# Handing a PSUM bank from one row tile to the other: GpSimd's empty instruction in place of SyncE's, and no weight split queued in the last six steps before it

## The chip, the cores and the metric

The kernel runs on one core of one Trainium2 chip. The metric is device time in microseconds (us); before the change it is 1293.22 us, the median of 3 runs (1291.1 to 1293.64). Five engines matter here: PE (TensorE, matmuls), DVE (VectorE), ACT (ScalarE), POOL (GpSimd) and SP (SyncE, which issues DMAs). Each takes its instructions in order; they wait for each other by semaphores.

## The reference

x is 2048 x 512; there are 32 heads of 16 with one shared key and value head, and a feed-forward net of width 1376. A gate mixes the two.

```python
g = _sigmoid((x * gate_w).sum(-1, keepdims=True))
q = (x @ wq) in 32 heads of 16;  k = x @ wk;  v = x @ wv     # one k and v for all heads
a = softmax(q k^T / 4) v, heads side by side, @ wo
b = (_gelu(x @ w_gate) * (x @ w_up)) @ w_down
return g * a + (1 - g) * b
```

## The kernel before

**Two streams of work on PE.** After a prologue (some 80 us: queries, keys, values), PE's order is written out by hand in `PLAN` (L45 to L108), one line for each job of the feed-forward net (`f`) or of the output projection (`w`). The letters interleave a job with attention. `S` and `Z` are scores: `scores` (L730) issues two matmuls into a pair of PSUM banks (L744), and ACT makes the exponential of the pair (L747). `Z` uses the third pair, which is also the bank of a job's first product `z`. `V` is the product of one step's probabilities with the values (`pv`, L809, matmuls in L815). `H` begins a job, `F` is one step of it, `R` ends it, `T` sends tanh to ACT.

**A job.** It makes two products at once, `z` and `y` (gate and up for a chunk of 128 of the 1376 columns, or two row blocks of the down or output projection). Every operand stands as a high and a low half, so a product has three terms for each piece of the contraction: a gate job has 12 terms, a down job 15 or 18, a `w` job 12. `pair_mm` (L509) walks through the terms twice: in the first half `z` takes rows 0 to 63 of each term and `y` rows 64 to 127, in the second half the other way round. So one step is two matmuls on the two row tiles of the array, side by side. There are 61 jobs: 39 gate jobs, 16 down jobs and 6 `w` jobs.

**The handover.** Between the halves each bank passes from one row tile to the other. PE must not begin the second half on a bank before the first half's matmuls have written it, so L522 to L526 put an empty instruction, the relay, on another engine: it waits (`after`, L506) for the last two matmuls of the first half, and the first two matmuls of the second half wait for it (L517, L518). It stands on SP. Whatever SP has been given earlier comes first in SP's queue.

**What SP issues in these stretches:** the weight loads of `fetch` (L345, `nc.sync.dma_start` in L349, 256 KB each into one of `STAGE` = 4 stage buffers `st`), the next query tile (`load_q`, L375: four DMAs in L367 and L368 and two in L373, called in L739 at the third key step of a unit), the reloads in L572 and the output (L628).

**Splits.** A weight part that has landed in `st` is split into halves by `split_part` (L352, L186, L187): VectorE casts the high half (`gh`, `dh`, `xh`), GpSimd subtracts it from the part (`gl`, `dl`, `xl`), and `fetch` then orders the next load, which needs a stage buffer that an earlier subtraction has freed. A gate job queues its parts in `todo` (`begin`, L578): two of the gate and up weights for a later job and one or two of the down weights, in the first jobs one of `wo` as well. The end of the last gate job of a row group queues four parts of x.

**Slots.** After every third step (`EVERY` = 3) `slot` (L490) takes one piece of waiting work into the instruction streams: with its argument true, the first of `todo`, or else the first of `bg`; with false, of `bg` alone. `bg` holds VectorE's work on finished attention units (`norm`, L750). In the first half all slots may take a split; in the second half there are slots up to four steps before its end.

Of the kernel before, what the change touches and what calls it, by code (L numbers as in the profile page):

```python
# [111 lines left out]
def mix_kernel(ctx, tc, xT, wq, wo, wf, out):  # L112
    nc = tc.nc
# [376 lines left out]
    def slot(split_too):  # L490
        for q in (todo, bg) if split_too else (bg,):
            if q:
                return q.pop(0)()
# [12 lines left out]
    def after(ins, name):  # L506
        tc.add_manual_dep(ins, name, SYNC, reason="a bank passes from one row tile to the other")

    def pair_mm(z, y, X, Y):  # L509
        for half in range(2):  # L510
            for q in range(len(X)):
                for j, (ps, (a, b)) in enumerate(((z, X[q]), (y, Y[q]))):
                    lower = (j + half) % 2
                    rs = slice(64 * lower, 64 * lower + 64)
                    mm = nc.tensor.matmul(ps, a[rs], b[rs], start=(half == 0 and q == 0),  # L515
                                          stop=(half == 1 and q == len(X) - 1), skip_group_check=True)
                    if half == 1 and q == 0:  # L517
                        after(mm.ins, relay[0])  # L518
                    if half == 0 and q == 0 and j == 0:
                        behind = [None, None]  # L520
                    behind[j] = mm.ins.name
                if half == 0 and q == len(X) - 1:  # L522
                    relay = nc.sync.nop(nofuse=True).ins  # L523
                    for name in behind:
                        after(relay, name)
                    relay = [relay.name]  # L526
                if q % EVERY == EVERY - 1 and (half == 0 or q + 4 <= len(X)):
                    slot(True)
                yield

    def weights_terms(n, t):
# [302 lines left out]
    def play(word, job):  # L834
        if job:
            X, Y = job[0]()
        for t in word.split():
            k = int(t[1:] or 1)
            if t[0] in "SZ":
                for _ in range(k):  # L840
                    score(t[0] == "Z")
            elif t[0] == "V":
                visit(k)
            elif t[0] == "T":
                advance(2)()
                for k, m in ((2, 1), (3, 0)):
                    defer(k, advance(m))
            elif t[0] == "H":
                advance(1)()
                z = two_banks("z", 2)[:, 0:TG]  # L850
                y = ps_f.tile([P, TG], F32, tag="pf", name="y")
                pairs = pair_mm(z, y, X, Y)
            elif t[0] == "F":
                for _ in range(k):
                    next(pairs)
            else:
                assert next(pairs, None) is None
                job[1](z, y)
# [72 lines left out]
```

## Time and profile before

| | before |
|---|---|
| time, median of 3 runs | 1293.22 us |
| the profiled execution | 1292.77 us |
| its span, first to last instruction | 1291.0 us |
| PE matmul busy | 1243.3 us |
| ACT busy | 1029.8 us |
| DVE busy | 571.1 us |
| POOL busy | 220.3 us |
| mean granted TensorE clock | 0.984 |

A row of a group of instructions gives line, engine, operation, output<-inputs and count, then busy time and the mean of one in ns, then the idle time of the engine ahead of them and what ended it. A row of the time line gives start and duration in us, and the idle time before it in brackets. SPq and POOLq are the sequencers of SP and GpSimd, which wait and issue. An empty instruction appears as EVENT_SEMAPHORE in its line, L523. A row of a view by stretches of time gives the stretch, its length, the busy time and count of each engine (PE, weight loads PEld, then DVE, ACT, POOL where they are not left out), the mean granted clock, and two numbers on the DMAs. The end of a matmul is modelled: a next one starts before the shown end of the one ahead.

### The profile page before, as it was taken

The page shows a single profiled execution, that of the slowest core. Times are in us where ns is not written, and L with a number is a line of the kernel's source. Part 1 is how long each engine was busy: PE and PEld are TensorE (multiplying, and loading weights), DVE is VectorE, ACT ScalarE, POOL GpSimd, SP SyncE. Part 2 cuts the span into 40 slices and gives each one's busy share as a digit, 9 for nine tenths or more (in the row PEclk, how much of TensorE's full clock was granted, in tenths as well). Part 3 has the DMA queues.
Part 4 walks back from the last instruction along what each step waited for, and adds up shares of the span by engine and source line. Part 5 has one row for each costly group of instructions (what it writes and reads, how often), then busy time and mean ns, then how long its engine had stood idle before and what let it go on. Part 6 is the DMA issues. An engine that isn't in the chain of part 4 may idle for free.

```text
span 1291.0 us, 23739 instructions
## 1 busy us (share of the span) xinstructions
PE 1243.3 (96%) x9742; PEld 683.6 (53%) x9742; DVE 571.1 (44%) x812; ACT 1029.8 (80%) x1127; POOL 220.3 (17%) x188
## 2 busy tenths in 40 slices
PE   9999999998999999999998999998999999999998
PEld 7864455545545545445554555455455544555555
DVE  7764423554246241264526234064635336053623
ACT  5448888777888878898787888887788888887883
POOL 5423101212022010121212011022202021012100
PEclk9999999989999999999999999999999999999999
DMA  8532101212021010111211121012212021012000
GB/s 317 204 125 66 52 7 50 62 39 79 9 77 49 30 55 22 38 46 42 79 55 46 39 63 31 22 50 63 63 39 63 30 71 47 1 47 60 17 1 33
DMA packets 39839, 73.91 MB, mean 57 GB/s; under 512 B 5488, under 2 KB 5744, under 8 KB 39728
## 3 DMA queue, kind: packets, MB, share of 16 engines
q1 hardware_dynamic: 39184, 71.32, 18.1%
q8 instruction: 77, 1.26, 0.4%
q0 software_dynamic: 256, 0.79, 0.2%
q14 instruction: 34, 0.28, 0.1%
q10 hardware_dynamic: 288, 0.26, 0.1%
HBM read 57.41 MB, written 14.94 MB: 56 GB/s over the span
## 4 chain that ended last, share of the span: by engine, by line
PE 69%; issue 16%; SPq 3%; POOL 1%; DVE 1%; POOLq 0%
PE acc L815 29%; PE s L744 17%; PE z L515 16%; PE y L515 7%; SPq L373 1%; POOL gl L187 1%; SPq L367 1%; SPq L368 1%; SPq L349 1%; PE wos L501 1%; DVE dh L186 0%; DVE acc L627 0%; POOL dl L187 0%; PE wof L501 0%; DVE gh L186 0%
## 5 line engine op out<-in xcount | busy, mean ns | idle before, releaser
L747 ACT ACTIVATE p<-s 128x1024 f32<-128x1024 f32 x1024 | 976.7, 1026 | 201.8 <-PE s L744 189.8
L815 PE MATMUL acc<-p,v 128*32 128x512 f32 x4096 | 484.8, 597 | 0.0
L744 PE MATMUL s<-Q,kp 51*128 51x512 f32 x2048 | 390.4, 421 | 1.5 <-DMA Q<-scr 1.4
L744 PEld LDWEIGHTS s<-Q,kp 51*128 51x128 f32 x2048 | 187.4, 187 | 218.7 <-ACT p L747 124.0
L187 POOL TENSOR_TENSOR gl<-st,gh 128x512 fp32r<-128x512 f32 x80 | 112.3, 1423 | 919.7 <-PE s L744 708.8
L815 PEld LDWEIGHTS acc<-p,v 128*32 128x32 f32 x4096 | 114.0, 109 | 250.2 <-issue 240.6
L515 PE MATMUL z<-xh,gh 64*128 64x512 f32 x312 | 131.4, 421 | 37.3 <-SPq L523 37.3
L515 PE MATMUL y<-xh,gh 64*128 64x512 f32 x312 | 131.3, 421 | 0.0
L515 PE MATMUL y<-xl,gh 64*128 64x512 f32 x312 | 127.5, 409 | 0.0
L515 PE MATMUL z<-xl,gh 64*128 64x512 f32 x312 | 127.4, 408 | 0.0
L515 PE MATMUL z<-xh,gl 64*128 64x512 f32 x312 | 126.8, 406 | 0.0
L515 PE MATMUL y<-xh,gl 64*128 64x512 f32 x312 | 126.8, 406 | 0.0
L541 DVE COPY gs<-z 128x512 f32<-128x512 f32 x39 | 27.0, 692 | 225.2 <-PE y L515 128.6
L515 PEld LDWEIGHTS z<-xh,gh 64*128 64x128 f32 x312 | 61.1, 196 | 56.6 <-SPq L523 47.8
L515 PE MATMUL z<-dh,hh 64*128 64x512 f32 x176 | 70.2, 399 | 3.7 <-SPq L523 3.7
L515 PE MATMUL y<-dh,hh 64*128 64x512 f32 x176 | 70.1, 398 | 0.0
L515 PE MATMUL y<-dl,hh 64*128 64x512 f32 x176 | 69.4, 394 | 0.0
L515 PE MATMUL z<-dl,hh 64*128 64x512 f32 x176 | 69.4, 394 | 0.0
L515 PE MATMUL z<-dh,hl 64*128 64x512 f32 x176 | 69.2, 393 | 0.0
L515 PE MATMUL y<-dh,hl 64*128 64x512 f32 x176 | 69.2, 393 | 0.0
L515 PEld LDWEIGHTS z<-xh,gl 64*128 64x128 f32 x312 | 60.8, 195 | 11.2
L515 PEld LDWEIGHTS z<-xl,gh 64*128 64x128 f32 x312 | 61.4, 197 | 9.8
(173 smaller groups left out, 1498.2 us busy)
## 6 DMA issues: line engine op xcount, KB each, us to landing
st<-wf SPq DMA_DIRECT2D x125, 256.0 KB
scr<-q SPq DMA_DIRECT2D x16, 512.0 KB
Q<-scr SPq DMA_DIRECT2D x64, 128.0 KB
Q<-scr SPq DMA_DIRECT2D x64, 64.0 KB
out<-acc SPq DMA_DIRECT2D x16, 256.0 KB
xr<-xT SPq DMA_DIRECT2D x6, 512.0 KB
st<-xT SPq DMA_DIRECT2D x12, 256.0 KB
xr<-xT SPq DMA_DIRECT2D x4, 256.0 KB
```

What stands on the lines that cost most here:

```text
L187: eng_l.tensor_sub(lo, src, hi)
L349: nc.sync.dma_start(t, source(*p))
L367: nc.sync.dma_start(t[64 * j : 64 * j + 32].bitcast(F32), rows[0:32, hs])
L368: nc.sync.dma_start(t[64 * j + 32 : 64 * j + KR].bitcast(F32), rows[0:16, hs])
L373: nc.sync.dma_start(Q[u][64 * j + KR : 64 * j + QK].bitcast(F32), shs[gb, a, :, j::2])
L501: nc.tensor.matmul(ps, a, b, start=(first and q == 0), stop=(last and q == len(terms) - 1), skip_group_check=True)
L515: mm = nc.tensor.matmul(ps, a[rs], b[rs], start=(half == 0 and q == 0), stop=(half == 1 and q == len(X) - 1), skip_group_check=True)
L541: nc.vector.tensor_copy(gs, g)
L744: nc.tensor.matmul(ps[:, j * TG : (j + 1) * TG], kp[rs, kc * P : (kc + 1) * P], Q[u][rs, pr], start=True, stop=True)
L747: nc.scalar.activation(p, ps, AF.Exp, bias=0.0, scale=SCALE)
L815: nc.tensor.matmul(accp[u][32 * j : 32 * j + 32], vt[:, kc], pb[s, j // 2][:, (j % 2) * TG : (j % 2 + 1) * TG], start=(kc == 0), stop=(kc ...
```

## The change

```diff
                 if half == 0 and q == len(X) - 1:
-                    relay = nc.sync.nop(nofuse=True).ins
+                    relay = nc.gpsimd.nop(nofuse=True).ins
                     for name in behind:
                         after(relay, name)
                     relay = [relay.name]
                 if q % EVERY == EVERY - 1 and (half == 0 or q + 4 <= len(X)):
-                    slot(True)
+                    slot(half == 1 or q + 6 <= len(X))
                 yield
```

The relay moves from SP's queue to GpSimd's. The slots of the first half that lie within its last six steps take from `bg` alone. In a job of 12 terms these are the slots after steps 9 and 12, so two splits stand in the first half in place of three or four; the third comes after step 3 of the second half. In a down job of 15 terms the slots after steps 12 and 15 are closed to splits.

Two places show it. The first is PE at the handover of the gate job of chunk 21 (the job of line 73 of the plan, the one at 610.6 us in the trace): the last two scores before the second half, and the first matmuls of that half, each with the semaphore that it waits for. Before:

```order
L744 MATMUL s<-Q_6182,kp 128x512 [waits Activation_49]
L744 MATMUL s<-Q_6182,kp 128x512
L515 MATMUL z<-xh_3503,gh_6377 128x512 [waits SP_sequencer_49]
L515 MATMUL y<-xh_3503,gh_6377 128x512
L515 MATMUL z<-xl_3504,gh_6377 128x512
```

After:

```order
L744 MATMUL s<-Q_6182,kp 128x512 [waits Activation_49]
L744 MATMUL s<-Q_6182,kp 128x512
L515 MATMUL z<-xh_3503,gh_6377 128x512 [waits Pool_sequencer_49]
L515 MATMUL y<-xh_3503,gh_6377 128x512
L515 MATMUL z<-xl_3504,gh_6377 128x512
```

PE's own order is the same; only the engine whose sequencer it waits for is another.

The second place is VectorE in the same job, from the copy of a finished attention unit (`n113` from `acc13`) to the copy of the job's product `z` (L541). The casts are those of three splits (`gh23` twice, `dh21`); L775 to L781 are the first four pieces of `bg`. Before:

```order
L769 COPY n113_6550<-acc13_6239 128x512
L186 CAST gh23_6565<-st_6381 128x512
L186 CAST gh23_6565<-st_6396 128x512
L186 CAST dh21_6604<-st_6413 128x512
L775 SCALAR_TENSOR_TENSOR nz12_6161<-n113_6550,mk_80,nz12_6161 128x512
L778 SCALAR_TENSOR_TENSOR n012_6160<-n113_6550,mkb_81,n012_6160 128x512
L772 STREAM_SHUFFLE n113_6550<-nz12_6161 128x512
L781 RECIPROCAL nz12_6161<-n113_6550 128x128
L541 COPY gs21_6670<-z_6557 128x512
```

After:

```order
L769 COPY n113_6550<-acc13_6234 128x512
L186 CAST gh23_6565<-st_6381 128x512
L186 CAST gh23_6565<-st_6396 128x512
L775 SCALAR_TENSOR_TENSOR nz12_6161<-n113_6550,mk_80,nz12_6161 128x512
L778 SCALAR_TENSOR_TENSOR n012_6160<-n113_6550,mkb_81,n012_6160 128x512
L186 CAST dh21_6629<-st_6436 128x512
L772 STREAM_SHUFFLE n113_6550<-nz12_6161 128x512
L781 RECIPROCAL nz12_6161<-n113_6550 128x128
L541 COPY gs21_6670<-z_6557 128x512
```

The cast of `dh21` now stands behind two pieces of `bg`; the list up to the z copy holds the same nine instructions. GpSimd's subtraction for `dl21` moves with it, behind the relay in GpSimd's queue, and so does the weight load that the split orders on SP.

## The prediction

> **What bounds the kernel now.** I read the page first, then the list of waits, then the time line of one job beside a job that stands under the same kind of plan line.
>
> ```profile
> span 1291.0 us, 23739 instructions
> PE 1243.3 (96%) x9742; PEld 683.6 (53%) x9742; DVE 571.1 (44%) x812; ACT 1029.8 (80%) x1127; POOL 220.3 (17%) x188
> ...
> L815 PE MATMUL acc<-p,v 128*32 128x512 f32 x4096 | 484.8, 597 | 0.0
> L744 PE MATMUL s<-Q,kp 51*128 51x512 f32 x2048 | 390.4, 421 | 1.5 <-DMA Q<-scr 1.4
> ...
> L515 PE MATMUL z<-xh,gh 64*128 64x512 f32 x312 | 131.4, 421 | 37.3 <-SPq L523 37.3
> ```
>
> PE is busy for 96% of the span, and its three big groups show idle time in one place only: ahead of the paired matmuls (L515), released by SP's empty instruction (L523). The list of waits gives the whole of it:
>
> ```profile
> PE z L515 <- SPq L523: 41.0, 18, 3.7
> ```
>
> So PE bounds the kernel, and 18 of the 61 handovers make it stand still, for 41.0 us together. This is how one looks: PE, then SP's DMA issues, in the job that begins at 610.6 us.
>
> ```profile
> 614.36 0.41 PE L744 MATMUL s<-Q,kp 51*128 51x512 f32 x2
> 617.52 0.50 PE L515 MATMUL z<-xh,gh 64*128 64x512 f32 x1 [2.75 <-SPq L523]
> ```
>
> ```profile
> 613.20 0.33 SPq L349 DMA_DIRECT2D st<-xT  x1
> 613.62 0.38 SPq L367 DMA_DIRECT2D Q<-scr  x1
> ...
> 615.45 1.49 SPq L373 DMA_DIRECT2D Q<-shs  x2
> 617.04 0.36 SPq L349 DMA_DIRECT2D st<-xT  x1
> ```
>
> PE has ended the first half by 614.8, but the empty instruction stands in SP's queue behind two weight loads (each waits until GpSimd's subtraction has freed a stage buffer) and six loads of the next Q (the first and the last two shown). SP is through with them at 617.40, and PE starts 0.12 us later. GpSimd and VectorE in the same job:
>
> ```profile
> 611.82 2.79 POOL L187 TENSOR_TENSOR gl<-st,gh 128x512 fp32r<-128x512 f32 x2 [15.36 <-PE s L744]
> 614.57 1.71 POOL L187 TENSOR_TENSOR dl<-st,dh 128x512 fp32r<-128x512 f32 x1
> ```
>
> ```profile
> 611.27 0.76 DVE L186 CAST gh<-st 128x512 fp32r<-128x512 f32 x2
> 611.93 1.52 DVE L186 CAST dh<-st 128x512 fp32r<-128x512 f32 x1
> ...
> 617.62 0.95 DVE L781 RECIPROCAL nz<-n 128x128 f32<-128x128 f32 x1
> 621.32 0.69 DVE L541 COPY gs<-z 128x512 f32<-128x512 f32 x1 [2.75 <-PE y L515]
> ```
>
> The stalls cost a second time. The granted clock is not 1 throughout, and the stretches at half clock lie just behind stalls. Below is the mean clock of the core, then stretches that I picked by stage, L515 alone (three of the eleven that I found at half clock, and the sum of all eleven), then a half that follows a stall at full clock.
>
> ```profile
> core 0: 1291.0 us, clock 0.984
> ```
>
> ```profile
> 87.10:90.50 3.40, 2.95 (x16) 1.98 (x14) 0.51 0.57 154
> ...
> 275.80:281.70 5.90, 5.43 (x24) 3.78 (x24) 0.50 0.30 94
> ...
> 544.50:547.90 3.40, 2.96 (x16) 2.01 (x14) 0.50 0.33 124
> ...
> sum 39.90, PE 35.08 PEld 23.69; mean PE 3.19 PEld 2.15
> ```
>
> ```profile
> 617.50:621.30 3.80, 3.55 (x24) 2.19 (x24) 1.00 0.74 198
> ```
>
> And the pace of PE, at full and at half clock:
>
> ```profile
> 600.42 0.40 PE L515 MATMUL z<-xh,gh 64*128 64x512 f32 x1
> ...
> 600.66 0.39 PE L515 MATMUL z<-xl,gh 64*128 64x512 f32 x1
> ```
>
> ```profile
> 545.71 0.63 PE L515 MATMUL z<-xh,gh 64*128 64x512 f32 x1
> ...
> 546.13 0.63 PE L515 MATMUL z<-xl,gh 64*128 64x512 f32 x1
> ```
>
> A step (one z and one y matmul side by side) takes 600.66 - 600.42 = 0.24 us at full clock, 0.42 us at half.
>
> **The change, part by part.** A change of 0.2%, about 2.6 us, is what a measurement of this kernel can tell from none.
>
> *The stalls go.* A matmul is shown for 0.40 us, but the next one may start 0.24 us after it, so each stall is 0.16 us longer than its idle time: 41.0 + 18 x 0.16 = 43.9 us. The new empty instruction stands in GpSimd's queue behind the first two splits' subtractions alone; the third split is now queued in the second half. Need it wait until those subtractions have run? The next two rows say no. They are line 187 in 613.3 to 614.0 us:
>
> ```profile
> L187 POOL TENSOR_TENSOR gl<-st,gh x1: 1468/1468/1468, 613.1 to 613.1; 128x512 fp32r<-128x512 f32 x1
> L187 POOLq EVENT_SEMAPHORE  x1: 15027/15027/15027, 613.5 to 613.5; - x1
> ```
>
> GpSimd's sequencer began its next wait at 613.5, while the second gl was running and dl, which comes ahead of that wait, had not begun (614.57). So the sequencer only needs the inputs of what stands ahead, and the last of these, the second gh cast, is done at 611.27 + 0.76 = 612.03, 2.7 us before PE ends the half. The empty instruction is then already waiting for PE, and only the hop is left. I take the residue as nothing in 17 stalls. The eighteenth is the first job, where the casts come late:
>
> ```profile
> 84.80 0.51 PE L744 MATMUL s<-Q,kp 51*128 51x512 f32 x2
> 86.69 0.50 PE L515 MATMUL z<-xh,gh 64*128 64x512 f32 x1 [1.39 <-SPq L523]
> ```
>
> ```profile
> L187 POOLq EVENT_SEMAPHORE  x3: 17/5823/12773, 79.0 to 85.1; - x3
> ```
>
> There (line 187, 84.8 to 86.0 us) the sequencer had passed the second gl at 85.1, and PE could have gone on at 84.80 + 0.24 = 85.04; with a hop, 0.3 us stay.
>
> *The hop itself* is not in this trace. SP's hop shows from below: PE started 0.12 us after SP's last DMA issue ended. From above I bound it by 0.1 us more for GpSimd than for SP in each of the 61 handovers, 6 us; from the other side by 0.05 us less, 3 us. I take nothing, being nearest to the SP row, for both are the same wait in a sequencer.
>
> *The clock comes back.* 39.9 us ran at half clock, in eleven stretches, each just behind or in a stall. There 0.42 us are spent on what takes 0.24: 39.9 x (1 - 0.24/0.42) = 17.1 us. The mean clock bounds it from above: (1 - 0.984) x 1291 = 20.7 us. From below it is nothing, if the cause is another. I take 18, between the two ends that rows give.
>
> [...]
>
> *The third split moves* from step 9 of the first half to step 3 of the second: one cast, one subtraction and one weight load a job. The cast and subtraction were off the critical path and stay in the same job; what hides them is the second half's PE work (617.52 to 621.32). The load is wanted a job later, over 10 us. VectorE's list up to the z copy is the same work in another order, ending at 617.62 + 0.95 = 618.57. The half would now end at 621.32 - 2.91 = 618.41, so the z copy comes 0.16 us late. Where a slow stretch goes too, as in the job at 543 us, its idle time is
>
> ```profile
> 548.55 0.69 DVE L541 COPY gs<-z 128x512 f32<-128x512 f32 x1 [4.30 <-PE y L515]
> ```
>
> ```profile
> 543.22 0.49 PE L515 MATMUL z<-xh,gh 64*128 64x512 f32 x1 [2.79 <-SPq L523]
> ...
> 548.68 1.07 PE L815 MATMUL acc<-p,v 128*32 128x512 f32 x8
> ```
>
> against 2.79 + 0.16 of stall and 3.4 x (1 - 0.24/0.42) = 1.5 of slow clock, so 0.15 us late as well. The plan puts at least one score (two matmuls) and one V (the last row, 1.07 us) between this and the next score in that bank; the copy takes 0.69 us, so this hides it. With that cover gone, and three times the 0.16 us at all 18: 9 us.
>
> *SP* loses its 61 waits; nothing of what it issues is needed sooner, so I count nothing.
>
> *What is late next?* The job before, with the same eight words "F3 S", had no stall. Its two halves, all engines:
>
> ```profile
> 593.50:597.50 4.00, 4.00 (x34) 3.19 (x34) 0.56 (x1) 4.00 (x5) 2.96 (x3) 1.00 0.45 132
> 597.50:601.30 3.80, 3.80 (x34) 2.94 (x32) 0.00 (x0) 3.76 (x5) 0.00 (x0) 1.00 0.27 73
> ```
>
> PE is busy throughout, and ACT (fourth column) too, without holding PE up. So a job without its stall runs at PE's pace, and nothing takes the stall's place.
>
> *Sum.* The profiled execution took 1292.77 us (span 1291.0 and 1.8 around it; the median shown is 1293.22). 1292.8 - 43.9 - 18 + 0.3 = 1231.2: I predict 1231.
>
> **The rivals.**
>
> 1. *The clock does not come back*: the half-clock stretches have another cause, and only the stalls go: 1292.8 - 43.9 + 0.3 = 1249. For it speaks that the stalls at 617.52 and some others had no slow stretch; against it, that no slow stretch stands without a stall. [...]
> 2. *GpSimd runs in order to the end*: the empty instruction waits until the subtraction ahead is done. The gl pair ends at 611.82 + 2.79 = 614.61, about where the half does, so most handovers lose 0.1 us, but the first job would wait for its pair, begun at 84.9, until some 87.7, 2.7 us, and have its slow stretch of 1.5 us. Together about 6 us over the forecast: 1237. The sequencer row at 613.5 speaks against it.
> 3. *VectorE becomes the bound* behind the stalls that go: 1231 + 9 = 1240. The idle of 2.75 us ahead of the z copy, no more than the stall, speaks for it; the V behind it against.
> 4. *Slower*: the second gh cast comes too late, so that the empty instruction stands behind a subtraction that waits for its input. In the list of waits GpSimd does wait so:
>
> ```profile
> POOL gl L187 <- DVE gh L186: 89.3, 7, 36.7
> ```
>
> In the job above the cast has 2.7 us in hand. Slower begins where the 39 gate jobs lose 62/39 = 1.6 us each, so where the cast came 4.3 us later everywhere. With 5.3 us it would be 1231 + 39 x 2.6 = 1332. Nothing new stands ahead of the casts in VectorE's order, so I give it little.
> 5. *The change does not do what it says*: something I don't see makes GpSimd answer as late as SP did, and the time stays at 1293.
>
> **How the numbers follow.** Forecast 0.74, its own range 1225 to 1238 (the hop's 3 us less and 6 us more, the clock's upper end, the spread of the runs) holding nine tenths of it. Rival 1 0.08, rival 2 0.06, rival 3 0.05, rival 4 0.04, rival 5 0.03. The forecast's own range with rivals 2 and 3 holds 0.78, so the range reaches to rival 1: 1225 to 1250, 0.86. Faster by over 0.2% is all but rivals 4 and 5: 0.93; the same 0.03; slower 0.04.
>
> **What would show it.** In the profile after: no wait of PE on L523 above 0.3 us, and the sum of such waits under 2 us, not 41.0; mean clock 0.99 or more; PE's share of the span at 99%, its busy time lower by the slow stretches; ACT near 84%; VectorE's z copies with idle time near nothing where stalls were. Half-clock stretches without stalls would show rival 1; waits of 1.3 us on L523, rival 2; new idle time ahead of L744 behind VectorE, rival 3; waits on L523 of several us, rivals 4 and 5, and then the forecast is wrong.

## The result, and the profile after

| | before | after |
|---|---|---|
| median | 1291.59 us (6 runs, 1289.43 to 1293.64) | 1230.87 us (6 runs, 1230.76 to 1230.99) |
| span of the profiled execution | 1291.0 us | 1229.0 us |
| PE matmul busy | 1243.3 us (96%) | 1222.3 us (99%) |
| ACT busy | 1029.8 us (80%) | 1025.8 us (83%) |
| DVE busy | 571.1 us | 545.5 us |
| mean granted clock | 0.984 | 1.000 |

The ratio is 0.953, with a 95% interval of 0.9518 to 0.9542: 4.7% faster. The predicted 1231 us is within 0.2 us of the median. The runs also spread less, over 0.2 us in place of 4.

These are the lines of the page after that answer to the ones shown of before: the engines, then the scores (L744) and the paired matmuls (L515), with their idle time behind the last bar.

```profile
span 1229.0 us, 23739 instructions
PE 1222.3 (99%) x9742; PEld 671.1 (55%) x9742; DVE 545.5 (44%) x812; ACT 1025.8 (83%) x1127; POOL 216.3 (18%) x188
...
L744 PE MATMUL s<-Q,kp 51*128 51x512 f32 x2048 | 385.3, 416 | 1.6 <-DMA Q<-scr 1.4
...
L515 PE MATMUL z<-xh,gh 64*128 64x512 f32 x312 | 125.7, 403 | 0.0
```

The 37.3 us of idle time ahead of the paired matmuls are gone, and the scores have no new idle time (1.5 us before). In the list of waits (total, times, longest, in us) the handover is left with weight loads alone. They run beside matmuls (671.1 us of weight loads and 1222.3 us of matmuls in a span of 1229.0 us), so a waiting weight load is not yet a waiting PE; no row of a waiting matmul names L523 any more:

```profile
PEld z L515 <- POOLq L523: 8.0, 26, 0.3
```

The mean clock of the core:

```profile
core 0: 1229.0 us, clock 1.000
```

And the job of chunk 21, which stood still for 2.75 us before, at its handover. PE, GpSimd, and the empty instruction itself (line 523 in 577 to 578.5 us):

```profile
577.54 0.41 PE L744 MATMUL s<-Q,kp 51*128 51x512 f32 x2
577.83 0.49 PE L515 MATMUL z<-xh,gh 64*128 64x512 f32 x1
```

```profile
575.00 3.06 POOL L187 TENSOR_TENSOR gl<-st,gh 128x512 fp32r<-128x512 f32 x2 [12.86 <-PE s L744]
579.03 1.30 POOL L187 TENSOR_TENSOR dl<-st,dh 128x512 fp32r<-128x512 f32 x1 [0.97 <-DVE dh L186]
```

```profile
L523 POOLq EVENT_SEMAPHORE  x1: 17/17/17, 577.8 to 577.8; - x1
```

The scores begin at 577.54 and the second half at 577.83, 0.29 us later, where the bare pace is 0.24. The empty instruction went off at 577.8, while the second gl was still running (to 575.00 + 3.06 = 578.06).

### The profile page after: what moved, and what is told of

Read it like the earlier page. It is cut to its first block, busy times and chain, and to the rows that moved or that the text cites. A ratio compares the mean times of both kernels' runs of the same rounds, so it can differ in the third digit from the quotient of the medians.

```text
span 1229.0 us, 23739 instructions
## 1 busy us (share of the span) xinstructions
PE 1222.3 (99%) x9742; PEld 671.1 (55%) x9742; DVE 545.5 (44%) x812; ACT 1025.8 (83%) x1127; POOL 216.3 (18%) x188
## 4 chain that ended last, share of the span: by engine, by line
PE 93%; DVE 0%; ACT 0%; DMA 0%; SPq 0%; issue 0%
PE acc L815 38%; PE s L744 23%; PE z L515 20%; PE y L515 11%; PE wos L501 1%; DMA Q<-scr 0%; DVE acc L627 0%; ACT p L747 0%; PE wof L501 0%; DVE sq L545 0%; DVE sq L544 0%; DVE gs L541 0%; ACT sq L548 0%; SPq L367 0%
## 5 line engine op out<-in xcount | busy, mean ns | idle before, releaser
L744 PE MATMUL s<-Q,kp 51*128 51x512 f32 x2048 | 385.3, 416 | 1.6 <-DMA Q<-scr 1.4
L744 PEld LDWEIGHTS s<-Q,kp 51*128 51x128 f32 x2048 | 184.2, 184 | 217.8 <-ACT p L747 125.1
L515 PE MATMUL z<-xh,gh 64*128 64x512 f32 x312 | 125.7, 403 | 0.0
L515 PE MATMUL y<-xh,gh 64*128 64x512 f32 x312 | 125.7, 403 | 0.0
L515 PE MATMUL y<-xl,gh 64*128 64x512 f32 x312 | 122.4, 392 | 0.0
L515 PE MATMUL z<-xl,gh 64*128 64x512 f32 x312 | 122.1, 391 | 0.0
L515 PE MATMUL z<-xh,gl 64*128 64x512 f32 x312 | 121.8, 390 | 0.0
L515 PE MATMUL y<-xh,gl 64*128 64x512 f32 x312 | 121.7, 390 | 0.0
L541 DVE COPY gs<-z 128x512 f32<-128x512 f32 x39 | 27.0, 692 | 194.8 <-PE y L515 125.5
L187 POOL TENSOR_TENSOR dl<-st,dh 128x512 fp32r<-128x512 f32 x44 | 57.3, 1304 | 127.4 <-PE s L744 88.8
L515 PE MATMUL z<-dh,hh 64*128 64x512 f32 x176 | 69.5, 395 | 0.0
L515 PE MATMUL y<-dh,hh 64*128 64x512 f32 x176 | 69.5, 395 | 0.0
L515 PE MATMUL y<-dl,hh 64*128 64x512 f32 x176 | 69.0, 392 | 0.0
L515 PE MATMUL z<-dl,hh 64*128 64x512 f32 x176 | 68.8, 391 | 0.0
L515 PE MATMUL y<-dh,hl 64*128 64x512 f32 x176 | 68.7, 391 | 0.0
L515 PE MATMUL z<-dh,hl 64*128 64x512 f32 x176 | 68.7, 391 | 0.0
L515 PEld LDWEIGHTS z<-xh,gh 64*128 64x128 f32 x312 | 58.0, 186 | 15.1 <-POOLq L523 6.8
L515 PEld LDWEIGHTS z<-xl,gh 64*128 64x128 f32 x312 | 58.3, 187 | 8.4
```

The costliest lines, as they stand in the source:

```text
L187: eng_l.tensor_sub(lo, src, hi)
L541: nc.vector.tensor_copy(gs, g)
L744: nc.tensor.matmul(ps[:, j * TG : (j + 1) * TG], kp[rs, kc * P : (kc + 1) * P], Q[u][rs, pr], start=True, stop=True)
```

## The experiments

Seven kernels, each against the changed kernel or the one before. "The theory" is that of the prediction: the long stalls came from what stood ahead of the relay in SP's queue, a sequencer passes a relay as soon as the inputs of what stands ahead are there, and the half-clock stretches were the stalls' second price.

**1. The relay alone.** The changed kernel with the slots as before:

```diff
-                    slot(half == 1 or q + 6 <= len(X))
+                    slot(True)
```

> The relay is on GpSimd, but splits may again be queued in all slots of the first half, so dl (and in a few jobs a fourth part) stands ahead of it. My theory (GpSimd's sequencer passes the relay once the inputs of what stands ahead are there, not once it has run): in the job at 610 us of the profile before, dl's cast was done 1.1 us before the half ended, so nearly nothing is lost; only the jobs with four parts lose up to 0.5 us each: 1231 to 1235 us, clock 0.99 or more. Rival (the relay waits until the subtraction ahead has run): dl ended 1.4 to 1.8 us after the half in 17 jobs of the profile before, so 17 x 1.6 = 27 us and some half-clock stretches: 1260 to 1275 us.

Measured: 1230.91 us (1230.62 to 1231.42), ratio to before 0.9535 (0.9514 to 0.9556), clock 0.999. That is the changed kernel's time. The same job there, GpSimd and PE:

```profile
577.92 1.75 POOL L187 TENSOR_TENSOR dl<-st,dh 128x512 fp32r<-128x512 f32 x1
```

```profile
577.71 0.41 PE L744 MATMUL s<-Q,kp 51*128 51x512 f32 x2
578.00 0.50 PE L515 MATMUL z<-xh,gh 64*128 64x512 f32 x1
```

dl stands ahead of the relay in GpSimd's queue and runs from 577.92 to 579.67. PE went on at 578.00, again 0.29 us behind the scores. So the relay did not wait for dl. (The expectation puts a fourth part ahead of the relay too; in the code the slot after a 12-term half's last step comes behind the relay, so three stood ahead.)

**2. The slots alone.** The relay back on SP, the slots as changed:

```diff
-                    relay = nc.gpsimd.nop(nofuse=True).ins
+                    relay = nc.sync.nop(nofuse=True).ins
```

> The relay stays on SP; only the slots of the last six steps are closed to splits. My theory (the relay stands behind the six loads of the next Q and the weight load before them): only the last weight load, 0.4 us, goes from in front of the relay, so 13 stalls of about 2.9 us become about 2.5 us, the four short ones nearly vanish, and most half-clock stretches stay: 1270 to 1288 us. Rival (the late third split made SP late): 1231 to 1236 us.

Measured: 1279.35 us (1276.64 to 1283.96), ratio 0.9909 (0.9874 to 0.9944), clock 0.987. The waits, then the job of chunk 21 on SP and PE:

```profile
PE z L515 <- SPq L523: 33.3, 14, 3.5
```

```profile
605.18 0.33 SPq L349 DMA_DIRECT2D st<-xT  x1
605.60 0.38 SPq L367 DMA_DIRECT2D Q<-scr  x1
...
607.43 1.49 SPq L373 DMA_DIRECT2D Q<-shs  x2
609.10 0.36 SPq L349 DMA_DIRECT2D st<-xT  x1
```

```profile
609.04 0.50 PE L515 MATMUL z<-xh,gh 64*128 64x512 f32 x1 [2.29 <-SPq L523]
```

The last weight load went behind the relay (609.10 is later than 609.04), and the idle time fell from 2.75 to 2.29 us, by about that load's issue. The four short stalls vanished: 14 waits in place of 18. The slots alone take some 11 us from 1290.7 us (the median of the kernel before, measured beside this run); that the six loads of Q hold the rest is what run 6 tests.

**3. Busy ahead of the relay.** In each job one more subtraction, held back until the last step but one, and queued ahead of the relay (`spare[-1]` is an idle tile `sq`; the lines that collect `spare` are left out):

```diff
+                if half == 0 and q == len(X) - 2:
+                    t = spare[-1]
+                    after(nc.gpsimd.tensor_sub(t, t, t).ins, behind[1])
                 if half == 0 and q == len(X) - 1:
                     relay = nc.gpsimd.nop(nofuse=True).ins
```

> As the changed kernel, and in each job one more subtraction on GpSimd (on an idle tile) ahead of the relay, which waits for the last step but one of the first half, so that it is running, 1.1 us from its end, when the half ends. My theory (the sequencer passes it): 1231 to 1234 us, no wait of PE matmuls on the relay. Rival (the relay waits until what is ahead has run): about 46 handovers have no more than two scores to cover it and lose about 1 us each: 1270 to 1285 us.

Measured: 1231.11 us in one run. The job of chunk 21: the extra subtraction (`sq`), PE, and the relay (now line 528, in 576.5 to 578.5 us):

```profile
578.29 1.49 POOL L526 TENSOR_TENSOR sq<-sq 128x512 f32<-128x512 f32 x1
```

```profile
578.11 0.50 PE L517 MATMUL z<-xh,gh 64*128 64x512 f32 x1
```

```profile
L528 POOLq EVENT_SEMAPHORE  x1: 17/17/17, 578.0 to 578.0; - x1
```

The relay went off at 578.0 and PE went on at 578.11, although the subtraction that stands ahead of the relay only began at 578.29. Over the whole run, 61 handovers, no matmul waited for the relay; the list of waits has weight loads alone, 0.3 us at the longest:

```profile
PEld z L517 <- POOLq L528: 8.2, 27, 0.3
```

This settles the second rival: GpSimd's relay waited neither for the end nor, in the job of chunk 21, for the start of what it follows.

**4 and 5. Stalls of a set length.** Here the relay is made to wait for one subtraction (and then for two) that begins when the first half is over; this is the run with one (the lines that collect `spare` are again left out):

```diff
+                    t = spare[-1]
+                    for _ in range(1):
+                        held = nc.gpsimd.tensor_sub(t, t, t).ins
+                    relay = nc.gpsimd.nop(nofuse=True).ins
+                    after(relay, held.name)
                     relay = [relay.name]
```

> As the changed kernel, but the relay is made to wait for one more subtraction that starts when the first half has ended: a stall of one subtraction, 1.3 to 1.4 us, in each of the 46 handovers without V behind them. My theory (half clock follows where a stretch of about 3.4 us on a fixed grid holds about 1.6 us of idle PE or more; 14 long stalls of the profile before fit that): 36 x 1.5 + 10 x 1.2 = 66 us from the stalls alone, about 1297 us, and clock 0.99 or more. Rival (any stall of over a us brings half clock): 46 x 1.5 us more, about 1366 us, clock about 0.88. Rival (the half-clock stretches have nothing to do with stalls): 1297 us as well.

> As the run with one extra subtraction, but with two (1.04 us each there), so about 2.3 us of idle PE in each of 47 handovers. From that run's 1.40 us a handover the stalls alone give 1231 + 47 x 2.44 + 4 = 1350 us. My theory (half clock follows a stretch of 3.41 us on a fixed grid that holds over 1.6 us of idle PE; a stall of 2.28 us puts that much into one stretch in (3.41 - 2.28 + 2 x 0.68)/3.41 = 73% of places): some 34 half-clock stretches of 1.5 us each, 51 us: about 1400 us, clock about 0.96. Rival (half clock has another cause than the stalls): 1350 us, clock 0.99.

Measured: 1304.41 us with one, 1407.72 us with two, each in one run; clock 0.993 and 0.958. The waits of PE, first with one subtraction, then with two:

```profile
PE z L517 <- POOLq L531: 58.3, 47, 3.9
```

```profile
PE z L517 <- POOLq L531: 117.0, 52, 5.0
```

With one, the stalls cost 58.3 + 47 x 0.16 = 66 us, as expected, and five stretches at half clock came on top, which the expected 1297 us did not hold: 1230.9 + 66 + 5 x 1.5 = 1304. The mean clock agrees: (1 - 0.993) x 1302.3 = 9 us of lost clock, where five stretches at half clock lose 5 x 3.41 / 2 = 8.5. With two, the stalls cost 117.0 + 52 x 0.16 = 125 us, and the records of the clock hold 34 stretches of 3.4 us: 1230.9 + 125 + 34 x 1.5 = 1407; here (1 - 0.958) x 1405.6 = 59 us of lost clock stand against 34 x 3.41 / 2 = 58. So stalls bring the half clock: without that, the second run would have taken 1350 us. But not every stall of over a us does, or the first run would have taken 1366 us. The half-clock stretches lie on a grid of 3.41 us: in the records of the clock before the change they begin at 87.14, 128.10 and 544.53 us, for instance, 12 and 134 steps from the first. How much idle time it takes shows in the first of the two runs, in stretches of its grid (all engines; PE's busy time is the first number behind the length, the granted clock the third from the end), and below them the stretch behind each (L517 alone, the clock again third from the end):

```profile
611.20:614.60 3.40, 1.74 (x16) 1.22 (x14) 3.40 (x5) 2.64 (x3) 3.07 (x2) 1.00 0.61 156
...
843.30:846.70 3.40, 1.89 (x16) 1.57 (x18) 3.32 (x5) 1.64 (x2) 2.70 (x2) 1.00 0.40 122
```

```profile
614.60:618.00 3.40, 2.96 (x14) 1.98 (x14) 0.50 0.61 128
846.70:850.10 3.40, 1.57 (x12) 0.80 (x10) 1.00 0.29 77
```

PE idle for 3.40 - 1.74 = 1.66 us: half clock next (0.50). Idle for 3.40 - 1.89 = 1.51 us: full clock (1.00). (The expectation says that all 14 long stalls before the change fit an edge of 1.6 us; the first job's, with 1.39 us of idle time and a clock of 0.51 behind it, does not.)

**6. No loads of Q.** The kernel before, without the query loads after the second:

```diff
     def load_q(u):
+        if u >= 2:
+            Q[u] = Q[u - 2]
+            return
```

> The kernel before, relay on SP and splits in all slots, without the loads of the query tiles after the second (the scores go on with the first two tiles, so that part of the attention is not computed). My theory (the six loads of the next Q ahead of the relay make the long stalls): the long stalls fall to the 0.5 us of the weight load alone, that is 16 x 0.5 + about 1.3 in a down job + 1.7 in the first job, 11 us over the changed kernel, and a half-clock stretch or none: 1236 to 1250 us. Rival (the weight loads, which wait for GpSimd, make them): the stalls stay at 2 us and more, 1270 to 1290 us.

Measured: 1240.88 us (1240.44 to 1242.14), ratio 0.9609 (0.9593 to 0.9625), clock 0.998. The waits of PE on SP's relay:

```profile
PE z L518 <- SPq L526: 5.6, 17, 0.8
```

With the relay still on SP and all splits where they were, the longest of these waits fell from 3.7 to 0.8 us. What is left is the weight load behind GpSimd's subtraction, about half a us at 17 handovers. The first job did not lose the 1.7 us of the expectation: its scores began at 86.33 and its second half at 86.96, 0.4 us over the bare pace. The profile's one half-clock stretch, at 81.6 us, lies ahead of that, behind 1.64 us in which PE waited for the first query tile and not for a relay; the mean clock of the profiled execution is 0.998.

**7. The relay on VectorE.**

```diff
-                    relay = nc.gpsimd.nop(nofuse=True).ins
+                    relay = nc.vector.nop(nofuse=True).ins
```

> As the changed kernel, with the relay on VectorE, which has casts and two pieces of 1.8 us ahead of it in the jobs that stalled. My theory (a sequencer passes a relay once the inputs of what stands ahead are there, on VectorE as on GpSimd): 1231 to 1240 us. Rival (VectorE's relay waits until what is ahead has run): in the job at 574 us of the profile after, the second piece ends 0.9 us after the half, so some 14 stalls of about 1 us and longer ones where a chain of pieces waits for itself: 1245 to 1275 us.

Measured: 1232.96 us in one run, with one wait of a matmul on L523, of 1.3 us, in the first job. The job of chunk 21 does not test the theory: the second of the two pieces stands behind the relay and not ahead of it, and so began only after the half (idle time in brackets, ended by PE):

```profile
576.90 1.78 DVE L775 SCALAR_TENSOR_TENSOR nz<-n,mk,nz 128x512 f32<-128x512 f32 x1
579.66 0.75 DVE L778 SCALAR_TENSOR_TENSOR n<-n,mkb,n 128x512 f32<-128x512 f32 x1 [0.98 <-PE y L515]
```

The first job does. There a cast (L556) and a subtraction that needs its result (L557) stand ahead of the relay:

```profile
85.02 1.49 DVE L556 CAST hh<-gs 128x512 fp32r<-128x512 f32 x1
86.55 1.65 DVE L557 TENSOR_TENSOR hl<-gs,hh 128x512 fp32r<-128x512 f32 x1
```

```profile
86.64 0.49 PE L515 MATMUL z<-xh,gh 64*128 64x512 f32 x1 [1.33 <-DVEq L523]
```

PE waited until the cast was done (85.02 + 1.49 = 86.51), but not for the subtraction, which ran until 88.20. So VectorE's sequencer too passed an instruction that was running, and what held the relay until 86.6 was the subtraction ahead, which lacked its input until 86.51. This is one handover, and in it the input's coming and the subtraction's start fall together; for GpSimd run 3 tells them apart.

## Why the prediction was right

*The stalls go* (43.9 us): no matmul waits for the relay any more. PE's idle time fell from 1291.0 - 1243.3 = 47.7 us to 1229.0 - 1222.3 = 6.7, by the 41.0 us of the list of waits. Run 6 shows whose they were, for without the Q loads they shrink to half a us with the relay still on SP; run 2 shows that the splits' place had the smaller part in them (some 11 us, clock included).

*GpSimd's sequencer does not wait for what runs ahead.* I read this off one row, a wait that began before dl did (613.5 against 614.57). Run 3 shows it directly (the relay at 578.0, the subtraction ahead of it at 578.29), run 1 in the kernel itself (PE at 578.00, dl until 579.67). So the second half of the change, no splits in the last six steps, buys nothing beside the first: 1230.91 us without it, 1230.87 with it.

*The clock comes back* (18 us, between 0 and 20.7): the clock is 1.000. The span fell by 62.0 us, of which 62.0 - 43.9 = 18 are left for it and the small terms. That the stalls caused the slow stretches is shown by runs 4 and 5, where stalls that I put in brought them back at 1.5 us each (mean clocks of 0.993 and 0.958). The kernel before varies in the same way: of the seven runs measured beside run 1, the slowest took 1293.49 us at a mean clock of 0.984 and the fastest 1288.37 us at 0.988.

*The hop* (nothing, up to 6 us): 0.29 us from the scores to the second half where nothing else covers it, 0.05 us over the bare pace. Over all handovers this is too small to be told from the other small terms of the sum.

*The first job* (0.3 us left): PE's time line has the scores at 84.85 and the second half at 85.27, so 85.27 - 84.85 - 0.24 = 0.18 us.

*One step was off, without a price.* I took VectorE's list up to the z copy as the same work in another order and of the same length, so that the z copy would come 0.16 us late where it had 2.75 us of idle time. It had 1.01 us left:

```profile
578.53 0.42 DVE L186 CAST dh<-st 128x512 fp32r<-128x512 f32 x1
...
579.66 0.95 DVE L781 RECIPROCAL nz<-n 128x128 f32<-128x128 f32 x1
581.62 0.69 DVE L541 COPY gs<-z 128x512 f32<-128x512 f32 x1 [1.01 <-PE y L515]
```

The cast of dh takes 0.42 us here and took 1.52 before. In its new place it begins after the gl pair is done (578.06), while before it ran beside that pair. Run 1, where it keeps its old place, shows what I had expected, a z copy with no idle time ahead of it:

```profile
575.29 1.52 DVE L186 CAST dh<-st 128x512 fp32r<-128x512 f32 x1
...
581.90 0.63 DVE L541 COPY gs<-z 128x512 f32<-128x512 f32 x1
```

So the moved split gives VectorE 24 us over the kernel (569.7 us busy in run 1, 545.5 after), and all of it lies in these casts: the 44 of dh take 62.0 us in run 1 and 37.6 us after. It is off the path that sets the end, and the two kernels take the same time.

Of the rivals, the clock that stays low falls with the clock of 1.000 and with runs 4 and 5, GpSimd in order to the end with run 3, and VectorE as the bound with the scores' idle time, which did not grow, and with run 1, where the z copy comes 0.1 us later behind the handover and the time is the same. Slower and no change fall with the time itself.

## What to carry to other kernels

In SP's queue, which issues DMAs, an instruction that only passes a semaphore on cost what stood ahead of it: each issue (0.33 to 0.43 us, and 1.49 us for the two of L373) and the wait for a buffer (with the weight load behind it about 0.5 us at 17 handovers of run 6). Put such an instruction on an engine whose queue holds, at that place, nothing that still waits for an input; that engine may be busy (shown for GpSimd in runs 1 and 3, where no matmul waited for the relay in 61 handovers, for VectorE in one handover of run 7). And count a PE stall with its second price: if it brings a half-clock stretch (run 5 had 34 of them), 1.5 us come on top of it.

## What the runs showed of the hardware

- In run 4, PE at rest for 1.66 us in one stretch of 3.4 us was followed by a stretch at half clock (0.50), and 1.51 us at rest by one at full clock (1.00). The edge is not sharp: the first job's stall before the change, 1.39 us of idle time, had half clock (0.51) behind it.
- GpSimd's sequencer let a relay go 0.3 us before the subtraction queued ahead of it had begun (run 3, 578.0 against 578.29).
- In run 7, VectorE's sequencer let a relay go while the subtraction queued ahead of it ran on for another 1.6 us (PE went on at 86.64, the subtraction ended at 88.20), but only once that subtraction's input was done (86.51).
- A cast of 128 x 512 on VectorE took 1.52 us beside GpSimd's subtractions (run 1, at 575.29) and 0.42 us without them (the changed kernel, at 578.53).
- Every kernel here hands the banks over by a relay; what PE would write without one was not shown.
